# Row sums of two head pairs in one PSUM bank, with spreading products of 64 rows

## The chip, the cores and the metric

The kernel runs on one core of a Trainium2 chip. The core's engines work side by side, each through its own list of instructions in order, and wait for one another by semaphores: TensorE (PE in the profile; PEld is its weight load), VectorE (DVE), ScalarE (ACT), GpSimd (POOL) and SyncE (SP), which here issues nearly all transfers. The metric is the device time of one execution in microseconds (us). Three runs of the kernel before took 552.09, 552.25 and 552.89 us; the median is 552.25.

## The reference, cut to what matters

```
scores = scale * q @ k.T ; scores = cap * tanh(scores / cap)      # 2 batches x 12 heads, 448 x 64 each
attn   = exp(scores - max)
attn   = attn / (attn.sum(-1) + 1e-9)                             # the row sums of this case
x      = (attn @ v), heads joined to 768 columns
x      = moe(x)      # rms norm, silu(x @ w_gate) * (x @ w_val) @ w_out
out    = moe2(x)     # x @ w_in, leaky max with alpha, @ w_out
```

All is float32. The change touches only the attention and its passage into the first matrix products: how the exponentials of a row are summed, how 1/sum gets back to the partitions of the heads, and the order around these.

## The kernel before, in words

Two heads make a pair; there are 12 pairs, and pair i is prepared, scored and summed by the loop `for i in range(NPAIR)`, whose passes are called turns here. Turn i holds, on TensorE: the scores of pair i (`qk`, L207; four score groups, of which the narrow last one comes first, then three with two heads on 64 rows each), the row sums of pair i-1 (`sums`, L249) and its product with v (`pv`, L236). Values are split in a rounded high part and a rest (`hi`, `lo`), so that each score takes three products. ScalarE does tanh (L216) and exp (L221) of pair i into the tile `pt`.

The exponentials lie with the keys on the partitions, so a row sum is a product with ones. `sums` makes eight products of 32 columns per pair, in four column groups that run beside each other: two rounds. The result stands in a PSUM bank of its own (`under()`), and VectorE copies it out (`us`, L272, the *u-copy*). Two small transfers (`gt`, L275) bring the sums of a pair to 32 partitions. For each two pairs `recip` (L284 to L291, tiles gf, th, tl) adds the parts, takes the reciprocal and splits it, and two transfers (L295) put it into the tile r. `norm` (L322) then spreads it by a product with `sel_t` to 128 partitions, and VectorE multiplies it into the copied output of the pair (`ee`, L264, the *o-copy*; `xf`, L323).

Other work is strewn over the turns by a table of (turn, step): `a` puts a step behind the exp of its turn, `z` behind the output product. Such steps are `prep` (L190, L191: hi and lo of the next pair), and the conversion of the first weights: `w_load` (L102, 768 KB), `w_top` (L113), `w_bits` (L118, here *bits*, which frees the buffer of a load and so lets the next load go out), `w_hi` and `w_lo` (L133, L139; wh, wl), and sums of two weight tiles on GpSimd (L126). GpSimd also squares the outputs for the rms norm (L306, L310); in turn 9 TensorE adds the squares of the first batch over the partitions (`rms_sum`, L339). All orders are written out by hand: each engine does its steps in the order in which the code issues them.

PSUM banks set some of the waits: the spreads write into the banks `u` and `o`; `o` is also that of the output product, so a spread there needs the o-copy of pair i-2 to be done.

Of the kernel before, what the change touches and what calls it, by code (L numbers as in the profile page):

```python
# [34 lines left out]
RP = 16  # L35
Q = 32
K3 = KD // 2
# [20 lines left out]
def attn_moe_kernel(ctx: ExitStack, tc: tile.TileContext, units, qk_in, v, sel, w, gvec, alpha, out):  # L58
# [22 lines left out]
    half = aconst.tile([P, 2, D], F32, name="half")  # L81
    sel_t = aconst.tile([P, 2, P], F32R, name="sel_t")
# [158 lines left out]
    def tiles_of(i):  # L241
        return [pt[i][:, min(n, TILES - 1)] for n in range(TILES + 1)]
# [171 lines left out]
    with tc.manual_schedule():  # L414
# [7 lines left out]
        for h in range(2):  # L422
            nc.vector.memset(half[h * D:h * D + D, h], 1.0)
# [922 lines left out]
```

## Time and profile before

| | |
|---|---|
| median of 3 runs | 552.25 us |
| profiled execution | 552.85 us, span 551.1 us |
| TensorE, VectorE, ScalarE, GpSimd busy | 99%, 81%, 67%, 18% of the span |
| attention, from the first score to the last output product | 4.56 to 100.64 us |
| TensorE's granted clock | full in all slices |

The profile is of one execution; its times count from the start of the span. Busy shares are an average: in the attention part VectorE and ScalarE are busier than over the whole span. A row of the timeline gives start, duration, engine, line, operation, the tiles written and read, and in brackets how long the engine stood idle before and what ended that. Consecutive instructions of one form are merged (x2 and so on).

### The profile page before, as it was taken

What the parts mean: (1) busy time and instruction counts of PE and PEld (TensorE: products, weight loads), DVE (VectorE), ACT (ScalarE), POOL (GpSimd) and SP (SyncE); (2) the same over time, 40 slices, a digit from 0 to 9 for tenths busy, and PEclk for the clock granted to TensorE, in tenths of its full rate; (3) what the DMA queues carried; (4) which work ended last, traced back from release to release, by engine and by line L of the source; (5) the groups of instructions that cost most, each with busy time, mean ns of one, the idle gap of its engine ahead of it and who ended that gap; (6) DMA issues with size and microseconds to landing.
All of it is one profiled execution on the core that took longest, in us unless ns stands there. A gap on an engine that the chain in (4) does not pass through costs nothing.

```text
span 551.1 us, 7691 instructions
## 1 busy us (share of the span) xinstructions
PE 545.6 (99%) x3061; PEld 461.3 (84%) x3061; DVE 448.5 (81%) x511; ACT 370.6 (67%) x433; POOL 98.8 (18%) x54
## 2 busy tenths in 40 slices
PE   8999999999999999999999999999999999999997
PEld 5444544699999999999999999999999999999996
DVE  4698889898999967878889898979866899999242
ACT  7989999477766554576757554787967996467110
POOL 0034663300065231010000048101111000000000
PEclk9999999999999999999999999999999999999999
DMA  7756420400334534065510573005512267013022
GB/s 253 260 188 197 164 73 8 163 12 1 120 120 162 178 110 171 1 228 173 184 46 1 229 230 114 1 0 173 172 58 69 105 203 255 0 59 115 0 101 100
DMA packets 17316, 66.09 MB, mean 120 GB/s; under 512 B 3584, under 2 KB 5504, under 8 KB 17280
## 3 DMA queue, kind: packets, MB, share of 16 engines
q1 hardware_dynamic: 16746, 65.08, 34.9%
q8 instruction: 24, 0.39, 0.3%
q10 hardware_dynamic: 390, 0.39, 0.2%
q0 software_dynamic: 144, 0.13, 0.1%
q14 instruction: 12, 0.10, 0.1%
HBM read 62.66 MB, written 2.75 MB: 119 GB/s over the span
## 4 chain that ended last, share of the span: by engine, by line
PE 96%; DVE 1%; ACT 1%; DMA 1%; issue 0%; DVEq 0%
PE s L395 19%; PE x L395 13%; PE m L395 13%; PE s L775 9%; PE s L749 8%; PE x L775 7%; PE oo L236 6%; PE s L207 5%; PE x L749 4%; PE m L775 4%; PE rps L249 3%; PE m L749 2%; PE s L408 1%; PE m L408 1%; PE x L408 1%; ACT pt L221 1%
## 5 line engine op out<-in xcount | busy, mean ns | idle before, releaser
L133 ACT CAST wh<-wt 128x768 fp32r<-128x768 f32 x105 | 87.1, 832 | 66.4 <-PE s L775 24.9
L139 DVE TENSOR_TENSOR wl<-wt,wh 128x768 fp32r<-128x768 f32 x108 | 113.6, 1053 | 12.5 <-ACT wh L133 12.2
L126 POOL TENSOR_TENSOR wt<-wt 128x768 f32<-128x768 f32 x33 | 75.1, 2284 | 265.9 <-DVE wt L118 97.9
L113 ACT CAST top<-raw 128x768 f16<-128x768 bf16 x64 | 68.8, 1076 | 27.0 <-DMA raw<-w_in 11.7
L118 DVE SCALAR_TENSOR_TENSOR wt<-raw,top 128x768 uint32<-128x768 uint32 x68 | 69.8, 1028 | 1.5 <-ACT top L113 1.5
L395 PE MATMUL s<-xx,wh 128*128 128x448 f32 x264 | 63.5, 364 | 0.0
L395 PEld LDWEIGHTS s<-xx,wh 128*128 128x128 f32 x264 | 49.4, 187 | 4.6 <-issue 0.7
L395 PE MATMUL x<-xx,wh 128*128 128x448 f32 x204 | 49.9, 366 | 0.0
L395 PE MATMUL m<-xx,wh 128*128 128x448 f32 x204 | 49.5, 364 | 0.0
L619 DVE TENSOR_TENSOR xx<-b,xx 128x896 fp32r<-128x896 f32 (+1 forms) x40 | 48.8, 1228 | 0.6 <-ACT xx L632 0.6
L216 ACT ACTIVATE pt<-s,cinv 128x896 f32<-128x896 f32 (+1 forms) x48 | 41.1, 911 | 6.2 <-PE s L207 5.9
L395 PEld LDWEIGHTS x<-xx,wh 128*128 128x128 f32 x204 | 38.2, 188 | 3.5 <-issue 0.4
L395 PEld LDWEIGHTS m<-xx,wh 128*128 128x128 f32 x204 | 38.2, 187 | 3.0
L775 PE MATMUL s<-xx,wh 128*128 128x448 f32 x132 | 40.0, 362 | 0.0
L236 PE MATMUL oo<-pt,vt 128*32 128x448 f32 x384 | 38.5, 540 | 0.4 <-ACT pt L221 0.3
L221 ACT ACTIVATE pt<-pt,cap_t 128x3136 f32<-128x3136 f32 (+2 forms) x13 | 35.3, 2714 | 0.4
L395 PE MATMUL s<-xx,wl 128*128 128x448 f32 x132 | 33.8, 364 | 0.0
L236 PEld LDWEIGHTS oo<-pt,vt 128*32 128x32 f32 x384 | 12.2, 110 | 23.6 <-issue 21.4
L775 PE MATMUL x<-xx,wh 128*128 128x448 f32 x104 | 31.2, 362 | 0.0
L749 PE MATMUL s<-xx,wh 128*128 128x448 f32 x96 | 27.2, 364 | 0.0
L775 PEld LDWEIGHTS s<-xx,wh 128*128 128x128 f32 x132 | 24.7, 187 | 2.1
L775 PE MATMUL s<-xx,wl 128*128 128x448 f32 x72 | 26.5, 367 | 0.0
(223 smaller groups left out, 1119.0 us busy)
## 6 DMA issues: line engine op xcount, KB each, us to landing
raw<-w_in SPq DMA_DIRECT2D x68, 768.0 KB
rw<-qk_in SPq DMA_DIRECT2D x11, 480.0 KB
vt<-v_in SPq DMA_DIRECT2D x12, 256.0 KB
out<-b SPq DMA_DIRECT2D x2, 448.0 KB
out<-b SPq DMA_DIRECT2D x2, 224.0 KB
out<-e SPq DMA_DIRECT2D x1, 448.0 KB
out<-c SPq DMA_DIRECT2D x2, 224.0 KB
gt<-us SPq DMA_DIRECT2D x23, 3.5 KB
```

What stands on the lines that cost most here:

```text
L113: copy(top_of[u].bitcast(F16)[:, 1::2], raw_t[u].bitcast(BF16)[:, 4:4 * n + 4:4])
L118: nc.vector.scalar_tensor_tensor(out=f_t[u].bitcast(U32), in0=raw_t.pop(u).bitcast(U32)[:, 1:2 * n + 1:2], scalar=13, in1=top_of.pop(u), o ...
L126: add(out=t, in0=f_t[a], in1=f_t[b], op=op)
L133: copy(h_t[u], f_t[u].rearrange("p (k m) -> p k m", m=P))
L139: nc.vector.tensor_tensor(out=l_t[u], in0=f_t[u].rearrange("p (k m) -> p k m", m=P), in1=h_t[u], op=ALU.subtract)
L216: nc.scalar.activation(out=t[:, 2 * g:2 * g + w], in_=st.pop((i, g))[:, :w, :S], func=AF.Tanh, scale=cinv)
L221: nc.scalar.activation(out=t[:, done:to], in_=t[:, done:to], func=AF.Exp, scale=cap_t)
L236: nc.tensor.matmul(oo[i][q * Q:q * Q + Q, :S], vv[:, n, q % 2 * Q:q % 2 * Q + Q], t[:, min(n, TILES - 1), :], start=c == 0, stop=c == TG, ...
L395: nc.tensor.matmul(ps[:, r, c0:c1], lhs, rhs[:, c0:c1], start=first and n == 0, stop=n == len(mm) - 1, skip_group_check=True,)
L619: nc.vector.tensor_tensor(out=out, in0=a, in1=b, op=op)
L749: nc.tensor.matmul(dst[m], wt[:, kk * MB + m, :], x, start=first and u == 0 and kk == 0 and n == 0, stop=u == 1 and kk == 1 and n == 2, sk ...
L775: nc.tensor.matmul(dst[m], wt[:, kk * MB + m, :], x, start=start and ks + kk == 0 and i == 0, stop=fin and last and kk == 1 and i == 2, sk ...
```

## The change

- `sums` works for two pairs. All row sums of two pairs stand in one bank: each product has 32 columns of a strip that is zero but for eight of them, so the four rows of head sums of a column group don't touch. For the even pair VectorE first adds tiles 0, 1 to tiles 2, 3 (`add_halves`, tile tp, 128x896); the first half of that takes part in the even pair's four products, the second half is the first of the odd pair's eight: 12 products for 16.
- The bank is copied out once per two pairs, in the turns with even i, and one transfer of 16 rows in 8 pieces each brings it to 128 partitions. `recip` folds these to 64 and then 32 partitions: seven VectorE instructions for four.
- 1/sum goes to rows 0, 32, 64, 96 (and the rest to 1, 33, 65, 97) of r, and a spread is a product over 64 rows. In the loop the first spread of a turn follows the narrow score group, in the second bank of that group's tile, the second follows the first wide score group.
- Places: recip stands ahead of prep in all turns (before: behind it in turns 3, 5 and 7); wh and wl of the first two weights stand in turns 4 and 5 (before 3 and 4); the loads of the second and third weight are issued in turn 1; behind the loop the last spreads come three products later, and three products of the next block come ahead of the sum of squares.

```diff
-RP = 16
+RP = 8
 Q = 32
+UNIT = Q // 4
...
+    def add_halves(i):
+        t = half_sum[i] = sb.tile([P, 2, S], F32, tag="tp", name="tp", bufs=1)
+        nc.vector.tensor_tensor(out=t, in0=pt[i][:, 0:2], in1=pt[i][:, 2:4], op=ALU.add)
 
     def sums(i):
 
-        us[i] = ps_s.tile([P, 2, 512], F32, tag="s", name="us")[:, 0] if i == NPAIR - 1 else under()
-        for n, t in enumerate(tiles_of(i)):
-            q = n % 2 * D + n // 2 % 2 * Q
+        n, j = group[i]
+        t, at_ = pt[i], lambda h: (0, 3 * UNIT - (2 * j + h) * UNIT)
+        tail = (t[:, TILES - 1], (1, 3 * UNIT - 2 * j * UNIT))
+        whole = [(t[:, c], at_(c % 2)) for c in range(TILES - 1)]
+        if j == 0:
+            row_sum[n] = under()
+            x = half_sum[i]
+            half_sum[i] = [(x[:, h], at_(h)) for h in range(2)]
+            steps = [*whole[4:], tail, half_sum[i][0]]
+        else:
+            steps = [half_sum.pop(i - 1)[1], *whole, tail]
+        for q, (x, (k, c)) in enumerate(steps):
+            q0 = q % 4 * Q
             nc.tensor.matmul(
-                us[i][q:q + Q, :S], half[:, n % 2, :Q] if n > 5 else ones[:, :Q], t, start=n < 4, stop=n > 3,
+                row_sum[n][q0:q0 + Q, :S], strip[:, k, c:c + Q], x, start=j == 0, stop=j == 1 and q > 3,
                 skip_group_check=True,
             )
...
+    def evac_u(n, queue=nc.sync):
+
+        gt[n] = sb.tile([4 * Q, S // RP], F32, tag="gt", name="gt", bufs=1)
+        u = sb.tile([P, S], F32, tag="us", name="us", bufs=1)
+        nc.vector.tensor_copy(u, row_sum.pop(n)[:, :S])
+        queue.dma_start(out=gt[n], in_=u[0:P:UNIT].rearrange("r (p s) -> r p s", p=RP))
...
+        nc.vector.tensor_copy(f, t[2 * Q:])
+        nc.vector.tensor_tensor(out=f, in0=t[:2 * Q], in1=f, op=ALU.add)
+        nc.vector.tensor_copy(t[m], f[Q:])
         nc.vector.scalar_tensor_tensor(
-            out=f[m], in0=t[m, 0], scalar=eps_t[m], in1=t[m, 1], op0=ALU.add, op1=ALU.add
+            out=f[m], in0=f[m], scalar=eps_t[m], in1=t[m], op0=ALU.add, op1=ALU.add
         )
...
+    def spread(i, rps):
+        n, j = group[i]
+        rows = slice(j * D, j * D + D)
+        nc.tensor.matmul(rps[:, :S], sel_t[rows], r2[n % 2][rows], start=True, stop=True, skip_group_check=True)
+
+    def scaled(i, rps):
         b, p = divmod(i, NP)
-        nc.tensor.matmul(rps[:, :S], sel_t[:, j, :], r2[n % 2], start=True, stop=True)
         nc.vector.tensor_tensor(out=xf[b][:, p, :], in0=ee.pop(i), in1=rps[:, :S], op=ALU.mult)
...
+            if i % 2 == 0:
+                (a if i else z)(i and i + 1, add_halves, i)
...
             if i % 2 == 1 and i > 2:
-                steps.insert(i < 9, (recip, (i - 3) // 2))
+                steps.insert(0, (recip, (i - 3) // 2))
...
-        for n, j in ((3, 0), (4, 1), (9, 6)):
+        for n, j in ((4, 0), (5, 1), (9, 6)):
...
             if i:
-                evac_u(i - 1)
+                if i % 2 == 0:
+                    evac_u((i - 1) // 2)
```

How VectorE's list reads now in turn 7, from the o-copy (ee) on. Before:

```order
L264 COPY ee<-oo 128x448
L190 CAST hi<-rw 128x960
L191 TENSOR_TENSOR lo<-rw,hi 128x960
L284 SCALAR_TENSOR_TENSOR gf<-gt,eps_t 64x28
L287 RECIPROCAL gf<-gf 64x28
L290 CAST th<-gf 64x28
L291 TENSOR_TENSOR tl<-gf,th 64x28
L118 SCALAR_TENSOR_TENSOR wt<-raw,top_95 128x768
L272 COPY us<-rps 128x448
```

And of the change:

```order
L278 COPY ee<-oo 128x448
L246 TENSOR_TENSOR tp<-pt 128x896
L293 COPY gf<-gt 64x56
L294 TENSOR_TENSOR gf<-gt,gf 64x56
L295 COPY gt<-gf 32x56
L296 SCALAR_TENSOR_TENSOR gf<-gf,eps_t,gt 32x56
L299 RECIPROCAL gf<-gf 32x56
L300 CAST th<-gf 32x56
L301 TENSOR_TENSOR tl<-gf,th 32x56
L191 CAST hi<-rw 128x960
L192 TENSOR_TENSOR lo<-rw,hi 128x960
L119 SCALAR_TENSOR_TENSOR wt<-raw,top_95 128x768
```

The half-sum add and recip (gf to tl) now come ahead of prep (hi, lo) and bits (wt); the u-copy (us) is gone from this turn.

VectorE's list at the passage from turn 5 to turn 6, from bits to the products xf. Before:

```order
L118 SCALAR_TENSOR_TENSOR wt<-raw,top_95 128x768
L272 COPY us<-rps 128x448
L264 COPY ee<-oo 128x448
L323 TENSOR_TENSOR xf<-ee,rps 128x448 x2
L190 CAST hi<-rw 128x960
```

And of the change:

```order
L119 SCALAR_TENSOR_TENSOR wt<-raw,top_95 128x768
L134 CAST wh<-wt 128x768
L140 TENSOR_TENSOR wl<-wt,wh 128x768
L278 COPY ee<-oo 128x448
L335 TENSOR_TENSOR xf<-ee,s 128x448
L335 TENSOR_TENSOR xf<-ee,rps 128x448
```

wh and wl stand where the u-copy stood, ahead of the o-copy (ee) of turn 6.

TensorE's list at the beginning of turn 6, from the output product of turn 5. Before:

```order
L236 MATMUL oo<-pt,vt 32x448 x16
L322 MATMUL rps<-r_1_93,sel_t 128x448
L207 MATMUL s<-hi 128x448
L207 MATMUL s<-hi,lo 128x448
L207 MATMUL s<-lo,hi 128x448
L322 MATMUL rps<-r_1_93,sel_t 128x448
L207 MATMUL s<-hi 128x448 x2
L207 MATMUL s<-hi,lo 128x448 x2
L207 MATMUL s<-lo,hi 128x448 x2
L207 MATMUL s<-hi 128x448 x2
```

And of the change:

```order
L237 MATMUL oo<-pt,vt 32x448 x16
L208 MATMUL s<-hi 128x448
L208 MATMUL s<-hi,lo 128x448
L208 MATMUL s<-lo,hi 128x448
L331 MATMUL s<-r_1_93,sel_t 128x448
L208 MATMUL s<-hi 128x448 x2
L208 MATMUL s<-hi,lo 128x448 x2
L208 MATMUL s<-lo,hi 128x448 x2
L331 MATMUL rps<-r_1_93,sel_t 128x448
L208 MATMUL s<-hi 128x448 x2
```

The two spreads (from r by sel_t) each moved behind the next score group; the first writes into a tile of scores.

## Rows read from the trace of the kernel before

**Rows 1.** The page, part 4: the chain that ended last, by engine.

```profile
PE 96%; DVE 1%; ACT 1%; DMA 1%; issue 0%; DVEq 0%
```

**Rows 2.** Busy us of each engine (operations), clock, DMA share, GB/s, by stretch.

```profile
32.11:40.01 7.90, 7.90 (x76) 3.96 (x72) 7.83 (x10) 6.37 (x6) 4.18 (x3) 1.00 0.56 191
...
87.92:95.40 7.48, 7.48 (x74) 3.56 (x70) 6.67 (x13) 7.26 (x7) 0.15 (x1) 1.00 0.03 4
...
28.81:95.53 66.72, 66.50 (x599) 31.18 (x592) 58.23 (x79) 61.13 (x50) 32.96 (x21) 1.00 0.39 124
```

**Rows 3.** Timeline, TensorE, turns 3 and 6: start us, duration us, then the instruction.

```profile
27.46 1.32 PE L249 MATMUL rps<-pt,ones 128*32 128x448 f32 x10
...
28.99 3.19 PE L236 MATMUL oo<-pt,vt 128*32 128x448 f32 x32
...
48.40 0.37 PE L322 MATMUL rps<-r,sel_t 128*128 128x448 f32 x1
```

**Rows 4.** Timeline, VectorE, turns 4 to 6.

```profile
39.53 0.56 DVE L133 CAST wh<-wt 128x768 fp32r<-128x768 f32 x1
...
41.00 0.62 DVE L264 COPY ee<-oo 128x448 f32<-128x448 f32 x1
41.53 0.65 DVE L190 CAST hi<-rw 128x960 fp32r<-128x960 f32 x1
...
43.29 0.23 DVE L284 SCALAR_TENSOR_TENSOR gf<-gt,eps_t 64x28 f32<-64x28 f32 x1
43.56 0.32 DVE L287 RECIPROCAL gf<-gf 64x28 f32<-64x28 f32 x1
43.91 0.17 DVE L290 CAST th<-gf 64x28 fp32r<-64x28 f32 x1
...
44.23 0.94 DVE L118 SCALAR_TENSOR_TENSOR wt<-raw,top 128x768 uint32<-128x768 uint32 x1
...
47.62 0.62 DVE L264 COPY ee<-oo 128x448 f32<-128x448 f32 x1 [1.92 <-PE oo L236]
```

**Rows 5.** Timeline, SyncE (loads), VectorE and GpSimd, turns 4 to 8.

```profile
38.59 0.33 SPq L102 DMA_DIRECT2D raw<-w_in  x1
...
52.25 1.75 DVE L118 SCALAR_TENSOR_TENSOR wt<-raw,top 128x768 uint32<-128x768 uint32 x1
54.03 0.33 SPq L102 DMA_DIRECT2D raw<-w_in  x1
...
58.96 0.24 DVE L284 SCALAR_TENSOR_TENSOR gf<-gt,eps_t 64x28 f32<-64x28 f32 x1 [0.44 <-DMA gt<-us]
...
60.95 3.65 POOL L126 TENSOR_TENSOR wt<-wt 128x768 f32<-128x768 f32 x2 [4.13 <-DVE wt L118]
64.55 0.94 POOL L306 TENSOR_TENSOR sq<-xf 128x448 f32<-128x448 f32 x1
...
68.90 1.76 POOL L310 TENSOR_TENSOR s<-s,sq 128x448 f32<-128x448 f32 x1
```

**Rows 6.** Timeline, GpSimd, TensorE and VectorE, turns 9 and 10.

```profile
70.62 5.43 POOL L126 TENSOR_TENSOR wt<-wt 128x768 f32<-128x768 f32 x3
71.65 0.99 PE L339 MATMUL ms<-s,ones 128*128 128x448 f32 x2
...
73.22 1.07 DVE L284 SCALAR_TENSOR_TENSOR gf<-gt,eps_t 64x28 f32<-64x28 f32 x1
...
74.68 1.40 DVE L290 CAST th<-gf 64x28 fp32r<-64x28 f32 x1
...
80.02 0.36 PE L207 MATMUL s<-hi,lo 128*128 128x448 f32 x1
```

**Rows 7.** Groups by line and shape: busy us, mean ns of one, idle before.

```profile
L619 DVE TENSOR_TENSOR xx<-b,xx 128x896 fp32r<-128x896 f32 x34 | 36.5, 1085 | 0.0
...
L349 DVE RECIPROCAL spare<-spare 128x448 f32<-128x448 f32 x2 | 5.9, 2946 | 0.4 <-ACT spare L346 0.4
```

**Rows 8.** Timeline, ScalarE, turn 9.

```profile
73.50 2.80 ACT L216 ACTIVATE pt<-s,cinv 128x896 f32<-128x896 f32 x3 [1.20 <-PE s L207]
```

More of the change, by code (lines that the diff above doesn't have):

```diff
@@ L510, in attn_moe_kernel @@
                 evac_o(i - 2)
-            if pairs:
-                norm(i - 4, under())
             if i:
                 home = {1: (ps_r, "u"), 2: (ps_o, "o")}.get(i)
-                qk(i, TG, home[0].tile([P, 1, 512], F32, tag=home[1], name="s") if home else third())
-            if pairs:
-                norm(i - 3, upper("rps"))
+                t = home[0].tile([P, 1, 512], F32, tag=home[1], name="s") if home else third()
+                qk(i, TG, t)
+                if pairs:
+                    norms(i - 4, t[:, 1])
             if i == 9:
@@ L525, in attn_moe_kernel @@
                 qk(i, g, two())
+                if pairs and g == 0:
+                    norms(i - 3, upper("rps"))
                 if (i, g) == (1, 0):
@@ L551, in attn_moe_kernel @@
         evac_o(last - 1)
-        norm(last - 3, third()[:, 0])
-        norm(last - 2, under())
+        both = third()
+        norms(last - 3, both[:, 0], both[:, 1])
         sums(last)
@@ L556, in attn_moe_kernel @@
             square(j)
-        evac_u(last, (nc.sync, nc.scalar))
+        evac_u(len(members) - 1)
         pv(last)
@@ L580, in attn_moe_kernel @@
         w_hi(("g", 0, "S1"))
-        product(pb[1], ("g", 1, "A12"), "B21", True, rows=(0,), span=range(6))
-        norm(last - 1, under())
-        norm(last, third()[:, 0])
+        product(pb[1], ("g", 1, "A12"), "B21", True, rows=(0,))
+        norms(last - 1, under(), third()[:, 0])
         square(last - 1)
@@ L588, in attn_moe_kernel @@
         lows(late)
-        product(pb[1], ("g", 1, "A12"), "B21", True, rows=(0,), span=range(6, 3 * K3))
         sum4("g", 1)
         product(pb[1], ("g", 1, "A12"), "B21", True, rows=(1,))
+        pa[0] = chain_pair()
+        product(pa[0], ("g", 0, "A11"), "B11", True, rows=(0,), span=range(3))
         rms_sum(B - 1, upper("ms"))
@@ L668, in attn_moe_kernel @@
             keep_part(d11, g, pb, lambda: h_of(g)[:, 2:])
-            pa[g] = chain_pair()
-            product(pa[g], ("g", g, "A11"), "B11", True, cuts={} if g else {(0, 4): SHORT})
+            if g:
+                pa[1] = chain_pair()
+                product(pa[1], ("g", 1, "A11"), "B11", True)
+            else:
+                product(pa[0], ("g", 0, "A11"), "B11", True, rows=(0,), span=range(3, 3 * K3), cuts={(0, 4): SHORT})
+                product(pa[0], ("g", 0, "A11"), "B11", True, rows=(1,))
         w_hi(("g", 1, "S1"))
@@ L1290 @@
         va[:, :, h * TAIL:(h + 1) * TAIL, 6 + h] = vp[:, :, h, MAIN:]
-    se = np.zeros((P, 2, P), f32)
+    se = np.zeros((P, P), f32)
     for r in range(4):
-        for base in (0, 32):
-            se[base + r, r // 2, (r % 2) * D:(r % 2) * D + D] = 1.0
+        for x in range(2):
+            se[r * Q + x, (r % 2) * D:(r % 2) * D + D] = 1.0
     def tiles(a):
```

57 lines of the change are left out of this document (24 added, 33 removed).

## The prediction

> **What bounds the kernel now.** I read the page's engine shares and its chain first, then the attention part turn by turn, then each engine's timeline there. TensorE ends the program, 96% of the chain [rows 1]; its clock is granted in full in every stretch that I use [rows 2]. So every microsecond taken from TensorE is worth one, as long as nothing else becomes late. In the attention part the others have little to spare: from 28.81 to 95.53 us (66.72 us) VectorE is busy for 58.23, ScalarE for 61.13 [rows 2]. VectorE's largest idle stretch, 1.92 us at 47.62, ends when TensorE's output product is done [rows 4]: VectorE waits for TensorE, but only just.
>
> **TensorE's own sum.** The row sums of one pair are eight products in four column groups, two rounds: from 27.46 to the output products at 28.99, 1.53 us [rows 3], so 0.76 a round. Two pairs now take 12 products, three rounds for four: 6 x 0.76 = 4.6 us less. A turn with two spreads lasts 7.90 us, one without 7.48 [rows 2]: 0.21 a spread. If the two halves of 64 rows run beside other work, one of each two vanishes: 6 x 0.21 = 1.25 us (nothing if they don't). Together 5.8 us, were TensorE alone.
>
> **What VectorE pays.** Six half-sum adds of 128x896 are new, 1.09 us each by the adds of that shape [rows 7]. The u-copy falls away six times, 0.53 us each by the o-copy, which moves as much (41.00 to the next start at 41.53 [rows 4]). recip has seven instructions for four: the old four take 0.94 us, from 43.29 to 44.23 [rows 4]; the three new ones are near its small ones, 0.2 each; the reciprocal runs over 56 columns for 28, by 2946 ns for 448 against 0.32 us for 28 [rows 4, 7] 0.18 more, the others 0.03 each. Recip costs 1.8 us, 0.85 more (bounds: 0.3, if the small ones overlap, and 1.2). From turn 3 to turn 11 that is 5 x 1.09 + 5 x 0.85 - 5 x 0.53 = +7.0 us, where VectorE had 8.5 us idle (66.72 - 58.23), all of it waits for others. This sum alone forbids most of the 5.8 us: a gain of 1.5 us would need a VectorE that never waits.
>
> **Where it waits: turns 3 to 6.** Turn 3 gives up wh and wl (39.53 to 41.00 [rows 4], 1.47) and the u-copy, and takes the half-sum and the longer recip: 2.0 against 1.95, no change. Turn 4 has wh and wl of another weight, no change either. So VectorE comes to the o-copy of turn 5 at 41.0, as before [rows 4]; TensorE, faster, has waited for it. Turn 5's list is then: o-copy 0.53, half-sum 1.09, recip, prep 1.76 (41.53 to 43.29), bits 0.9, wh and wl 1.5 (moved here). Recip can't start before the transfer of the row sums has landed. That sits behind a weight load of 768 KB on SP's queue: the load of turn 6 was issued at 54.03, the transfer right behind it, and gf could start only at 58.96, having waited for it [rows 5]: 4.9 us after the load's issue. In turn 5 (load at 38.59) that allows 43.5, and the list is there at 42.6. So 43.5 + 1.8 + 1.76 + 0.9 + 1.5 = 49.4; I take 49.2, since in turn 5 of before gf started 4.7 after that load and did not wait [rows 4, 5]. The o-copy of turn 6 stood at 47.62 [rows 4]: +1.6. The second spread writes the bank that this copy empties; it moves from 48.40 [rows 3] to 50.0. The score group that used to follow it is done by then (-0.65): turn 7 starts at 55.38 + 1.6 - 0.65 = 56.3, 0.95 late. The transfer itself I price at the old one: one issue for two, 128 pieces for 64.
>
> **Turns 6 to 9.** After that o-copy VectorE's list is as before, so turn 6's bits end at 54.00 + 1.6 = 55.6, and the load goes out there. Recip of turn 7 now stands ahead of prep, and waits until 55.6 + 4.9 = 60.5, though VectorE is free at 58. Before, prep filled this time, and gf waited 0.44. Behind the waiting recip stand prep (hi and lo of pair 8, which TensorE needs at the start of turn 8) and bits, for which GpSimd waits. Recip ends at 62.3, prep at 64.05, bits at 64.95. TensorE wants lo at 56.3 + 6.72 + 0.3 = 63.3: 0.75 wait. Turn 9 then starts at 63.0 + 0.75 + 7.69 = 71.45 (before 70.74). GpSimd takes its two weight sums after these bits, then the squares of pairs 4 and 5: from 60.95 to 70.66, 9.7 us [rows 5], and TensorE's sum of squares in turn 9 needs the last of them. It came at 71.65, 1.0 after they were done [rows 6]. Now they end at 64.95 + 0.1 + 9.7 = 74.75, while TensorE is there at 72.35: 2.4 us wait (bounds: 0.1, if VectorE's prep and bits don't hold GpSimd up as they did before: its two sums take 3.65 and an undisturbed operation on squares 0.94 [rows 5], 3.65 + 4 x 0.94 = 7.4 for 9.7; 3.2, if the transfer of 128 pieces lands 0.8 later).
>
> **Turn 9 to the end.** In turn 9 VectorE copies the sum of squares and then has the half-sum and recip while GpSimd runs three weight sums (5.43 us). There gf took 1.07 us and th 1.40, against 0.23 and 0.17 undisturbed [rows 4, 6]: each waited until GpSimd's operation was over, 2.06 us in all. With GpSimd starting at 74.75, the half-sum goes at its first gap, 76.55 to 77.65; recip then takes 1.8 plus such waits. Two catches of a whole weight sum would be 3.6 us, none 0; I take the nearest row, 2.06. Prep ends at 77.65 + 1.8 + 2.06 + 1.76 = 83.3. TensorE's second score product of turn 10, at 80.02 before [rows 6], would come at 74.75 + 8.37 - 0.76 - 0.31 = 82.05: it waits to 83.3, +3.3 us.
>
> The Trainium skill ("SBUF — State Buffer", section "SBUF: two separate sides") says that VectorE and GpSimd share a port pair as an exclusive lock, taken also by a VectorE operation with two SBUF inputs, the loser blocking fully. The two rows of turn 9 agree (1.40 us against 0.17). By this rule the half-sum, which has two SBUF inputs, the first copy and the sum of recip would each lose to a weight sum, 3.6 us for my 2.06, and the time would be 1.5 us more than forecast; no row shows a copy of this size.
>
> From there: +0.6 (the second spread of turn 10 waits for an o-copy behind prep, bits 0.9 and wh 0.6), -0.2 (spreads), -0.76 (turn 11's sums), +0.5 of it back (ScalarE is busy 7.26 us in turn 11 [rows 2], and TensorE's turn would last 6.72), -0.2 and -0.2 for the last two pairs of spreads. 3.3 + 0.6 - 0.2 - 0.76 + 0.5 - 0.4 = +3.0. What follows keeps its places against TensorE; the three products put ahead of the last sum of squares fill what the later spread leaves, and I cost them at nothing (up to 0.6 if the last recip lands late). The profiled execution had 552.85 us (span 551.1), 0.6 above the median 552.25; its stretches are those of any run, so I add to the median: **555.3 us**.
>
> **Rivals.** *ScalarE is the only limit (chance 0.15).* If VectorE swallows its work, ScalarE's idle time bounds the gain: 66.72 - 61.13 = 5.6 us, of which 1.7 stays (1.20 in turn 9 behind the sum of squares [rows 8], and 0.5 of starts). 552.25 - 3.9 = 548.4. For it: TensorE's rounds go for certain. Against it: the 7.0 us of VectorE.
> *VectorE keeps pace, nothing gained (0.2).* The lag of turn 7 stands, but GpSimd's squares run unhindered in 7.4 us, and turn 9's wait goes, and some 0.4 of the catches with it: +3.0 - 2.4 - 0.4 = +0.2, 552.45 us. Against it: VectorE has the same hi, lo and bits to do among the squares.
> *The port decides (0.15).* Both small operations lose to a weight sum: +1.5, 556.8 us. It decides if recip of turn 9 starts before GpSimd's third sum does.
> *The change doesn't do what it says:* spreads of 64 rows do not overlap; then 1.25 us of TensorE's sum is missing, most of it hidden behind VectorE's waits, and 0.4 us is added. It is inside the range.
>
> **Numbers.** The forecast has 0.5. A measurement here can tell 0.2%, 1.1 us, from no change: faster is the first rival, 0.15; within is the second, 0.2; slower is the forecast and the third, 0.65. The range leaves out most of the first rival and a tail above the third: 551.0 to 557.6; the forecast's own is 553.6 to 556.4.
>
> **What would show it.** Right: recip's first copy in turn 7 waits 2 us or more on the transfer; TensorE waits on VectorE at the second spread of turn 6, on lo at turns 8 and 10, and on GpSimd at turn 9's sum of squares for over 1 us; rounds of row sums halve in odd turns. Wrong: recip finds its transfer landed; GpSimd's squares end ahead of turn 9; ScalarE without gaps through turns 5 to 11. Then the first rival holds.

## The result, and the profile after

The changed kernel takes 558.86 us (median of 4 runs, 558.30 to 559.01) against 552.17 before (4 runs, 552.02 to 552.89). By the medians it is 6.7 us slower, where 3.05 were forecast. The ratio on record is 1.0114, 95% interval 1.0101 to 1.0126, which is a loss of 5.6 to 7.0 us. Its profiled execution had 559.01 us and a span of 557.2; that of before 552.85 and 551.1. The spans differ by 6.1 us, and the account below explains these 6.1.

The page of the changed kernel: busy time, the clock in 40 slices, the chain [rows 1].

```profile
PE 545.3 (98%) x3013; PEld 460.0 (83%) x3013; DVE 458.6 (82%) x530; ACT 370.6 (67%) x433; POOL 99.6 (18%) x54
PEclk9999989999999999999999999999999999999999
PE 83%; DVE 8%; DMA 3%; ACT 2%; POOL 2%; issue 1%; DVEq 0%
```

TensorE held 96% of the chain, now 83%: VectorE, GpSimd and transfers have a share of it now. Up to turn 7 the steps came within 0.6 us of the forecast. Three rows of the timeline after (start, duration, instruction, idle before): the second spread of turn 6 waits for the o-copy (forecast start 50.0); ScalarE waits in that turn for the scaling, that is, for VectorE's product xf from the spread in the score tile, which was not in the forecast; and recip of turn 7 waits for its transfer (forecast 60.5).

```profile
49.46 0.46 PE L331 MATMUL rps<-r,sel_t 64*128 64x448 f32 x1 [1.19 <-DVE ee L278]
49.96 3.33 ACT L217 ACTIVATE pt<-s,cinv 128x448 f32<-128x448 f32 x4 [2.26 <-DVE xf L335]
60.14 0.19 DVE L293 COPY gf<-gt 64x56 f32<-64x56 f32 x1 [1.24 <-DMA gt<-us]
```

GpSimd's row of turns 8 and 9 answers to [rows 5, 6]: two weight sums, the squares (the last one is shown), three weight sums.

```profile
64.77 4.05 POOL L127 TENSOR_TENSOR wt<-wt 128x768 f32<-128x768 f32 x2 [6.83 <-DVE wt L119]
73.44 1.12 POOL L319 TENSOR_TENSOR s<-s,sq 128x448 f32<-128x448 f32 x1
74.53 6.23 POOL L127 TENSOR_TENSOR wt<-wt 128x768 f32<-128x768 f32 x3
```

The squares end at 74.56 (forecast 74.75, before 70.66), the weight sums at 80.76 (before 70.62 + 5.43 = 76.05 [rows 6]). VectorE in turn 9: the copy of the sum of squares, the half-sum, the first three of recip's seven steps, prep.

```profile
75.68 0.62 DVE L542 COPY spare<-ms 128x448 f32<-128x448 f32 x1 [2.98 <-PE ms L356]
76.22 1.08 DVE L246 TENSOR_TENSOR tp<-pt 128x896 f32<-128x896 f32 x1
77.33 1.70 DVE L293 COPY gf<-gt 64x56 f32<-64x56 f32 x1
79.07 1.77 DVE L294 TENSOR_TENSOR gf<-gt,gf 64x56 f32<-64x56 f32 x1
80.87 0.18 DVE L295 COPY gt<-gf 32x56 f32<-32x56 f32 x1
...
82.25 0.64 DVE L191 CAST hi<-rw 128x960 fp32r<-128x960 f32 x1
82.93 1.16 DVE L192 TENSOR_TENSOR lo<-rw,hi 128x960 fp32r<-128x960 f32 x1
```

The first two steps of recip take 1.70 and 1.77 us, though they take 0.19 and 0.21 in turn 7, where GpSimd rests; below, a step held like this is called *caught*. The third passes 0.1 us after GpSimd is done, and with it five steps (1.4 us) remain. In the kernel before, prep of pair 10 began here:

```profile
76.22 0.65 DVE L190 CAST hi<-rw 128x960 fp32r<-128x960 f32 x1
```

So prep is 6.03 us late. TensorE after: the sum of squares of turn 9, which waits for GpSimd's last square, the second score product of turn 10 (80.02 before [rows 6]), the first product behind the loop.

```profile
74.62 1.02 PE L356 MATMUL ms<-s,ones 128*128 128x448 f32 x2 [1.82 <-POOL s L319]
84.14 0.48 PE L208 MATMUL s<-hi,lo 128*128 128x448 f32 x1 [0.63 <-DVE lo L192]
106.09 1.04 PE L412 MATMUL s<-xx,wh 128*128 128x448 f32 x3
```

Before, that product started at 100.64: +5.45. Behind it to the end of the span there are 451.11 us, before 450.46: +0.65. Together 6.1, the difference of the spans. From prep to that product, busy us of the five engines, clock, DMA share, GB/s, after and then before:

```profile
82.25:106.09 23.84, 22.31 (x195) 8.79 (x187) 23.33 (x34) 20.20 (x19) 8.33 (x6) 1.00 0.06 16
```
```profile
76.22:100.64 24.42, 24.23 (x226) 9.88 (x219) 22.76 (x33) 21.50 (x19) 8.58 (x6) 1.00 0.07 14
```

Before, TensorE filled this stretch (24.23 of 24.42); after, VectorE does (23.33 of 23.84). The whole loss is thus 6.03 of late prep, less 0.58 in turns 10 and 11, plus 0.65 behind the loop. What made prep late took 18 more kernels to settle, because the first answers were wrong.

### The profile page after: what moved, and what is told of

Same layout as the page of the kernel before. It is cut to its first block, busy times and chain, and to the rows that moved or that the text cites. A ratio compares the mean times of both kernels' runs of the same rounds, so it can differ in the third digit from the quotient of the medians.

```text
span 557.2 us, 7578 instructions
## 1 busy us (share of the span) xinstructions
PE 545.3 (98%) x3013; PEld 460.0 (83%) x3013; DVE 458.6 (82%) x530; ACT 370.6 (67%) x433; POOL 99.6 (18%) x54
## 4 chain that ended last, share of the span: by engine, by line
PE 83%; DVE 8%; DMA 3%; ACT 2%; POOL 2%; issue 1%; DVEq 0%
PE s L412 18%; PE x L412 12%; PE m L412 12%; PE s L803 9%; PE s L777 8%; PE x L803 7%; PE x L777 4%; PE m L803 3%; PE m L777 2%; PE oo L237 1%; PE s L425 1%; ACT pt L217 1%; ACT pt L222 1%; DVE lo L192 1%; DVE hi L191 1%
## 5 line engine op out<-in xcount | busy, mean ns | idle before, releaser
L127 POOL TENSOR_TENSOR wt<-wt 128x768 f32<-128x768 f32 x33 | 76.3, 2321 | 268.5 <-DVE wt L119 100.6
L412 PEld LDWEIGHTS s<-xx,wh 128*128 128x128 f32 x264 | 49.3, 187 | 5.0 <-issue 0.9
L412 PE MATMUL s<-xx,wl 128*128 128x448 f32 x132 | 33.9, 365 | 0.0
L412 PE MATMUL x<-xx,wl 128*128 128x448 f32 (+1 forms) x104 | 26.6, 365 | 0.0
L412 PEld LDWEIGHTS s<-xx,wl 128*128 128x128 f32 x132 | 24.7, 188 | 2.2 <-DVE wl L140 0.3
```

What stands on the lines that cost most here:

```text
L127: add(out=t, in0=f_t[a], in1=f_t[b], op=op)
L412: nc.tensor.matmul(ps[:, r, c0:c1], lhs, rhs[:, c0:c1], start=first and n == 0, stop=n == len(mm) - 1, skip_group_check=True,)
```

## The experiments

Each kernel is the changed one with the edit shown. The table gives, from each run's trace, the end of GpSimd's weight sums of turns 8 and 9 (where they stand there), the start of prep of pair 10, the first product behind the loop, the span, and the median time with its ratio to before. The trace is of one execution, the time the median of 4 (11 in c6 and c7). Output products are named by their pair: that of pair n runs in turn n+1, and where an expectation says "the output product of turn 8", it is that of pair 8.

| run | sums end | prep | product | span | time, ratio |
|---|---|---|---|---|---|
| before | 76.05 | 76.22 | 100.64 | 551.1 | 552.2 |
| after | 80.76 | 82.25 | 106.09 | 557.2 | 558.86, 1.0114 |
| e1 | 79.96 | 81.46 | 105.26 | 556.4 | 558.36, 1.0114 |
| e2 | 80.65 | 82.14 | 106.06 | 557.1 | 558.79, 1.0115 |
| e3 | 79.24 | 80.73 | 104.57 | 555.7 | 557.12, 1.0086 |
| e4 | moved | 79.26 | 107.14 | 558.1 | 560.29, 1.0148 |
| e5 | 79.62 | 81.12 | 105.05 | 556.1 | 559.04, 1.0115 |
| e6 | 80.39 | 76.38 | 107.81 | 558.6 | 560.33, 1.0135 |
| e7 | 82.43 | 83.91 | 108.62 | 559.7 | 561.75, 1.0171 |
| e8 | 79.71 | 81.20 | 106.64 | 557.4 | 557.81, 1.0096 |
| e9 | 81.68 | 82.93 | 106.91 | 558.0 | 559.71, 1.0138 |
| e10 | 80.59 | 82.10 | 106.96 | 558.0 | 560.85, 1.0156 |
| c1 | 78.61 | 80.39 | 108.09 | 559.2 | 560.69, 1.0148 |
| c2 | 80.93 | 82.43 | 109.97 | 561.0 | 562.44, 1.0183 |
| e11 | moved | 79.28 | 104.78 | 559.7 | 560.73, 1.0141 |
| c3 | moved | 77.11 | 100.94 | 554.4 | 556.57, 1.0076 |
| c4 | 74.50 | 77.34 | 101.17 | 554.6 | 558.02, 1.0092 |
| c5 | 74.55 | 76.25 | 100.14 | 555.1 | 556.00, 1.0064 |
| c6 | 74.89 | 76.60 | 100.46 | 551.5 | 552.93, 1.0011 |
| c7 | 74.28 | 75.99 | 99.84 | 550.9 | 552.61, 1.0006 |

The first theory was: recip ahead of prep, the transfer behind the load, then TensorE's wait in turn 9 and the half clock that followed it. Theory 2, from e5 on, was: VectorE's own row of turn 9 ahead of prep sets the end, whatever is won before. The rivals are VectorE's added work as such (1) and ScalarE's waits for the scaling (2). Of the times that the theory under test led one to expect, only that of e3 came true; e5 and c6 missed theirs by 0.1 and 0.4 us, the others by more.

**e1.** Recip behind prep in turns 3 to 7.
```diff
-                steps.insert(0, (recip, (i - 3) // 2))
+                steps.insert(i < 9, (recip, (i - 3) // 2))
```


> Theory (the order around turns 7 to 9 costs most of it: the reciprocal chain ahead of prep waits 1.24 us for its transfer and itself takes about 2, so lo is written at 63.8, the weights' bits at 64.7, GpSimd's squares end at 74.6, TensorE waits 1.8 us in turn 9 and then runs at half clock for some 1.6 us): with the reciprocal chain behind prep in turns 3, 5 and 7, lo of turn 8 is there 2 to 3 us earlier, the wait of 1.8 us in turn 9 shrinks below 0.7, the granted clock stays at full, and the time falls by 2.5 to 4 us to about 555.5 us. Rival 1 (VectorE has 7 us more to do, wherever the chain stands): the wait moves to another place, 558 to 559.5 us. Rival 2 (ScalarE waits for the scaling of the first spread in turns 4, 6 and 8, since that spread lies in the score tile): no change, 558.9 us.


TensorE's wait in turn 9 fell from 1.82 to 0.41 us, as expected; the time did not follow (558.36).

**e2.** Eight products of ones in TensorE's wait.
```diff
-                rms_sum(0, upper("ms"))
+                ms = upper("ms")
+                for _ in range(8):
+                    nc.tensor.matmul(ms[:, :P], ones, ones, start=True, stop=True)
+                rms_sum(0, ms)
```


> Eight 128x128 products of ones are put ahead of turn 9's sum of squares, into its bank, where TensorE waits for GpSimd; nothing else is changed. Theory (of the 6.7 us, 1.6 are the half clock that follows this wait): the wait remains, but the granted clock stays near full from 74.6 to 79, the score products behind it run at 0.20 instead of 0.375 us, and the time falls by 1.2 to 1.8 us to about 557.3 us. Rival 1 and rival 2 (VectorE's work, ScalarE's waits): the work behind is due to other engines anyway, 558.6 to 559.2 us.


The clock stayed full in turn 9, and the half clock came in turn 10 instead, behind a wait of 1.52 us for hi (columns as above):
```profile
76.00:77.00 1.00, 1.00 (x14) 0.92 (x12) 1.00 (x2) 0.66 (x1) 1.00 (x2) 1.00 0.16 55
...
86.00:87.00 1.00, 1.00 (x9) 1.00 (x7) 0.69 (x2) 0.59 (x2) 0.54 (x1) 0.50 0.00 0
```
The output product of pair 8 came 1.7 us earlier, that of pair 9 0.9 later; the end did not move. So the half clock of turn 9 is not what makes prep late. That it costs nothing is not shown: of the changed kernel's four executions, the one whose mean granted clock was 1.000 took 558.30 us, the three below that 558.79 to 559.01; in e2 itself three at 1.000 took 558.37 to 559.02, the profiled one (0.996) 558.87.

**e3.** The weight load of even turns behind the row sums' transfer.
```diff
-                    a(i, w_next, conv[i - 2])
+                    (a if i % 2 else z)(i, w_next, conv[i - 2])
```


> In even turns the 768 KB weight load is issued behind the transfer of the row sums, instead of ahead of it. Theory: the reciprocal chains of turns 5 and 7 no longer wait 0.6 to 1.2 us for that transfer; in turn 7 the squares end some 1.2 us earlier, turn 9's wait falls from 1.8 to about 0.6 us and the clock may stay: 556 to 557.8 us. Rival 1 (VectorE's work as such): what the chain no longer waits it is late for otherwise, 558.5 to 559.2 us. Rival 2: 558.9 us.


1.5 to 1.7 us faster, the only early edit that paid. Recip of turn 9 was caught again, prep began at 80.73:
```profile
75.79 1.71 DVE L293 COPY gf<-gt 64x56 f32<-64x56 f32 x1
77.53 1.77 DVE L294 TENSOR_TENSOR gf<-gt,gf 64x56 f32<-64x56 f32 x1
...
80.73 0.64 DVE L191 CAST hi<-rw 128x960 fp32r<-128x960 f32 x1
```

**e4.** GpSimd's three weight sums of turn 8 in turn 10.
```diff
-        for put, n, fn, g in ((z, 6, sum1, 0), (z, 7, sum1, 1), (z, 7, sum2, 0), (a, 8, sum2, 1), (a, 8, sum3, 0),
-                              (z, 8, sum3, 1), (z, 10, sum4, 0)):
+        for put, n, fn, g in ((z, 6, sum1, 0), (z, 7, sum1, 1), (z, 7, sum2, 0), (z, 10, sum2, 1), (z, 10, sum3, 0),
+                              (z, 10, sum3, 1), (z, 10, sum4, 0)):
```


> GpSimd's three weight sums of turn 8 (6.2 us, 74.5 to 80.8) are put into turn 10, so that the reciprocal chain of turn 9 meets none of them. Theory (the two small operations that took 1.70 and 1.77 us in place of 0.19 and 0.21 were caught by these sums): they take 0.2 us each, the second score product of turn 10 starts 1 to 3 us earlier than 84.14, and the time falls by 0.6 to 2.5 us to about 557.5 us; if the sums in turn 10 catch other work there, half of it comes back. Rival 1 and rival 2: 558.7 to 559.2 us.


Recip of turn 9 was free (first row), the half-sum and recip of turn 11 were caught in its place, and TensorE waited for the rows they make:
```profile
77.41 0.19 DVE L293 COPY gf<-gt 64x56 f32<-64x56 f32 x1
...
93.48 2.44 DVE L246 TENSOR_TENSOR tp<-pt 128x896 f32<-128x896 f32 x1
95.95 1.72 DVE L293 COPY gf<-gt 64x56 f32<-64x56 f32 x1
```
```profile
102.09 0.47 PE L331 MATMUL s<-r,sel_t 64*128 64x448 f32 x2 [2.16 <-DMA r<-tl]
```

**e5.** wh and wl back in turns 3 and 4.
```diff
-        for n, j in ((4, 0), (5, 1), (9, 6)):
+        for n, j in ((3, 0), (4, 1), (9, 6)):
```


> wh and wl of the first two weight units are back where they were, in turns 3 and 4. Theory 2 (formed after the first four runs, in which turns 7 and 8 were won by up to 3 us and turn 9 gave nearly all of it back: VectorE's own row of turn 9, with the copy of the sum of squares, the half-sum add and the seven steps of the reciprocal chain ahead of prep, ends last and sets turn 10, whatever the turns ahead gain): the o-copy of turn 6 is 1.5 us earlier and ScalarE's wait of 2.26 us there goes, yet the end moves by 0 to 0.7 us only, 558.2 to 558.9 us. Rival 2 (ScalarE's waits): 1.5 to 2.3 us faster, 556.6 to 557.4 us.


Nothing in the median (559.04), though prep came 1.1 us earlier in the profiled execution. That one had 558.15 us at full clock; the other three (mean clock 0.996 to 0.997) had 558.85 to 559.46.

**e6.** Recip behind prep in every turn.
```diff
-                steps.insert(0, (recip, (i - 3) // 2))
+                steps.insert(1, (recip, (i - 3) // 2))
```


> The reciprocal chain stands behind prep in turns 5, 7, 9 and 11 alike (turn 9's stood ahead of it in both kernels). Theory 2: in turn 9 prep starts at about 76 instead of 80.8 to 82.3 us, TensorE no longer waits for lo in turn 10, the output product of turn 9 starts at 86.5 to 88 instead of 89.5 to 90 us, and the time falls by 2 to 3.5 us to about 556 us; should the spreads of turn 10 then wait for the two rows (they land some 2 us behind the chain's end), up to 1 us of it comes back. Theory 1 with rivals (VectorE's work as such, ScalarE's waits): as the run with the chain of turn 9 left ahead, 558.4 us.


Now prep was caught, and the first spread of turn 10 waited for the rows of recip:
```profile
76.38 2.30 DVE L191 CAST hi<-rw 128x960 fp32r<-128x960 f32 x1
78.71 2.69 DVE L192 TENSOR_TENSOR lo<-rw,hi 128x960 fp32r<-128x960 f32 x1
```
```profile
85.61 0.71 PE L331 MATMUL s<-r,sel_t 64*128 64x448 f32 x1 [3.47 <-DMA r<-tl]
```
Prep, caught in recip's place, ended 1.0 us behind GpSimd (81.40 against 80.39).

**e7.** No spread in the score tile.
```diff
-                    norms(i - 4, t[:, 1])
+                    pass
...
-                if pairs and g == 0:
-                    norms(i - 3, upper("rps"))
+                if pairs:
+                    norms(i - 4 + g, upper("rps"))
```


> Both spreads of an even turn go, one behind the first and one behind the second pair of score products, into the o bank; the score tile holds scores alone, so that its tanh waits for no scaling. Theory 2: ScalarE's waits of 1.48, 2.26 and 1.21 us in turns 4, 6 and 8 go, but turn 9 sets the end: 558 to 559.5 us. Rival 2 (these waits cost the time): 556 to 557 us. Against both, TensorE may wait at the second spread until the first is scaled, some 0.6 us in each of four turns: then 559 to 561 us.


ScalarE's waits for the scaling went, and the kernel was 2.9 us slower. By itself this does not refute rival 2, since the new place has a price of its own: TensorE waited 1.39 us at a spread of turn 6 for the o-copy, ScalarE 1.46 us for scores in that turn. What refutes it as the main cause is c6 below, where the waits for the scaling are still 2.47, 0.46 and 1.13 us in turns 4, 6 and 8 (changed kernel: 1.48, 2.26 and 1.21) and 5.9 us are back.

**e8.** The half-sum adds left out; TensorE's passes take a tile of ones.
```diff
-        t = half_sum[i] = sb.tile([P, 2, S], F32, tag="tp", name="tp", bufs=1)
-        nc.vector.tensor_tensor(out=t, in0=pt[i][:, 0:2], in1=pt[i][:, 2:4], op=ALU.add)
+        if i == 0:
+            half_sum["t"] = sb.tile([P, 2, S], F32, tag="tp", name="tp", bufs=1)
+            nc.vector.memset(half_sum["t"], 1.0)
+        half_sum[i] = half_sum["t"]
```


> The six half-sum adds (1.08 us each, more where GpSimd is busy) are left out: TensorE's passes take a tile of ones in place of the half sums, so that the row sums are other numbers; all else is the same. Theory 2 and rival 1 (VectorE's work): VectorE's row of turn 9 is 1.1 us shorter, that of the turns ahead too, and the time falls by 3 to 5.5 us to about 554.5 us. Rival 2 (ScalarE's waits): 0 to 1.5 us less. If the time falls below 552.4 us, the saved passes are worth what TensorE's rows say (5.8 us) and the adds alone turned the gain into a loss.


Six adds gone, 1.0 us faster in the median (557.81; the intervals of the two ratios overlap); prep again 1.49 us behind the sums. The work of the adds alone is not the loss. The profiled execution was the slowest of the four (559.18): TensorE ran at half clock from 85 to 91 us (one row; columns as in e2), and the product came 25.44 us behind prep in place of 23.84. The one at full clock took 556.69 us, 1.6 less than the changed kernel's at full clock (558.30).
```profile
86.00:87.00 1.00, 1.00 (x9) 0.39 (x9) 0.97 (x3) 1.00 (x3) 1.00 (x2) 0.50 0.00 0
```

**e9, e10.** In e9 the weight sums of turn 7 stand behind the squares; in e10 the copy of the sum of squares stands behind recip.
```diff
-        for put, n, fn, g in ((z, 6, sum1, 0), (z, 7, sum1, 1), (z, 7, sum2, 0), (a, 8, sum2, 1), (a, 8, sum3, 0),
+        for put, n, fn, g in ((z, 6, sum1, 0), (a, 8, sum1, 1), (a, 8, sum2, 0), (a, 8, sum2, 1), (a, 8, sum3, 0),
```
```diff
+        def keep_ms():
+            rms_keep(0)
+            nc.vector.tensor_copy(rstd[0], ms_of[0][:, :S])
+            ms_of[0] = rstd[0]
...
+            if i == 9:
+                steps.insert(1, (keep_ms,))
...
-                rms_keep(0)
-                nc.vector.tensor_copy(rstd[0], ms_of[0][:, :S])
-                ms_of[0] = rstd[0]
```


> GpSimd's two weight sums of turn 7 stand behind the squares of turn 8 instead of ahead of them; all else as in the changed kernel. Theory 2, now sharper: VectorE's copy of the sum of squares stands at turn 9's head and waits 3 us for GpSimd's squares; the half-sum add, the reciprocal chain and prep are queued behind it, so that lo of turn 10 is late by what the squares are late. Expected: the squares end near 71.5 instead of 74.6 us, neither TensorE (1.82 us) nor VectorE (2.98 us) waits for them, prep of turn 10 starts near 79.5 instead of 82.25 us, and the time falls by 2 to 3.5 us to about 556 us. Theory 1's first form (the clock and the wait of turn 9 are the cost): 1.8 to 3.4 us less as well, but with prep of turn 10 still past 81.5. Rivals 1 and 2: 558.3 to 559.3 us.

> VectorE's copy of the sum of squares stands behind the reciprocal chain of turn 9 and ahead of prep; GpSimd's order is as in the changed kernel, so that TensorE still waits 1.8 us for the squares. Theory 2: the half-sum add and the chain run in VectorE's idle 3 us (from 72.7 us), prep of turn 10 starts 2 to 3 us earlier, near 79.5 us, and the time falls by 1.5 to 3 us to about 556.5 us although TensorE's wait and the half clock behind it stay. Theory 1's first form: 558.3 to 559.3 us, since that wait is untouched.


Both slower. In e9 five weight sums ran on end, and three steps of recip were caught after the half-sum:
```profile
71.83 9.85 POOL L127 TENSOR_TENSOR wt<-wt 128x768 f32<-128x768 f32 x5
```
```profile
74.36 2.05 DVE L246 TENSOR_TENSOR tp<-pt 128x896 f32<-128x896 f32 x1
76.44 1.73 DVE L293 COPY gf<-gt 64x56 f32<-64x56 f32 x1
78.20 1.78 DVE L294 TENSOR_TENSOR gf<-gt,gf 64x56 f32<-64x56 f32 x1
80.02 1.71 DVE L295 COPY gt<-gf 32x56 f32<-32x56 f32 x1
```
In e10 recip began 3.0 us earlier (74.31), four steps were caught, and its last step came only 0.7 us earlier. Theory 2 falls: it is not recip's start that counts; GpSimd's last sum lets it end. The late copy brought a wait of its own, since the output products of pair 8 need that bank:
```profile
82.23 3.21 PE L237 MATMUL oo<-pt,vt 128*32 128x448 f32 x32 [1.41 <-DVE spare L487]
```

**c1, c2.** e3, e5 and e10 together; with e9 besides.


> Three edits at once: the row sums' transfer ahead of the weight load, wh and wl back in turns 3 and 4, the copy of the sum of squares behind the reciprocal chain. Theory 2: what the first two win ahead of turn 9 (1.5 and 1 to 1.5 us) is no longer eaten there: the output product of turn 8 starts near 76 us, that of turn 9 near 86, and the time is 552.5 to 555 us. If turn 9 is set by something that none of the three touches: above 556 us.

> The three edits of the run before and the squares ahead of the weight sums of turn 7. Theory 2: TensorE waits nowhere over 1 us in turns 8 to 10, its clock stays at full, the output product of turn 9 starts near 84.5 us, as in the kernel before, and the time is 550.5 to 553 us, level with the kernel before or a little faster. If VectorE's added 7 us of work are the limit by themselves (rival 1): 554 to 557 us.


Both slower. The wait of the output products of pair 8 for the late copy grew to 4.1 and 6.6 us. Read together, the table had by then the answer: prep started 1.25 to 1.51 us behind the end of the sums in ten of the eleven traces with the sums there and recip ahead of prep (c1, with its copy in between, 1.78). The first product behind the loop came 23.80 to 23.98 us behind prep in after, e1, e2, e3, e5 and e9, with 3 to 4 us at half clock in between (e1, e2, e3, e9) or none; it took longer in e7 (24.71), in e8 with its half clock (25.44), and in e10, c1 and c2 with the wait for the bank (24.86 to 27.70). Theory 3 is: each small step of recip passes only once per weight sum, so GpSimd's last sum sets recip's end, prep, and what follows.

**e11.** One of the three sums in turn 10, two behind the loop.
```diff
-        for put, n, fn, g in ((z, 6, sum1, 0), (z, 7, sum1, 1), (z, 7, sum2, 0), (a, 8, sum2, 1), (a, 8, sum3, 0),
-                              (z, 8, sum3, 1), (z, 10, sum4, 0)):
+        for put, n, fn, g in ((z, 6, sum1, 0), (z, 7, sum1, 1), (z, 7, sum2, 0),
+                              (z, 10, sum2, 1), (z, 10, sum4, 0)):
...
         sum4("g", 1)
+        sum3("g", 0)
+        sum3("g", 1)
```


> Of GpSimd's three weight sums of turn 8 one goes behind the squares of turn 10 and two behind the loop's end, past the last reciprocal chain; all else as in the changed kernel. Theory 3 (read from ten traces: prep of turn 10 starts 1.5 us behind the end of GpSimd's weight sums in all of them that have these sums there, whatever was done ahead, since each small step of the reciprocal chain passes only once per weight sum): the chain of turn 9 takes 1.9 instead of 4.9 us, prep starts near 79.3 instead of 82.25, the second score product of turn 10 near 80.6 instead of 84.14, turn 11's chain meets no sum either (in the run with all three in turn 10 it did), and the time falls by 2 to 3.5 us to about 556 us. Theory 2 (the copy of the sum of squares and the half-sum add ahead of it): 0 to 1 us less.


Prep at 79.28, as expected, but the product behind the loop only 1.3 us earlier, and 3.8 us were lost behind it; the time, about 556 expected, was 560.73.

**c3, c4, c5.** e3, e5 and e11 together (c3); the two sums of turn 7 behind the squares besides (c4); no half-sums for pairs 8 and 10 besides, 14 passes there (c5).


> That edit, the row sums' transfer ahead of the weight load, and wh and wl back in turns 3 and 4. Theory 3: with the chain of turn 9 free of GpSimd, what the other two win ahead of it (1.5 us and 1 us) stays: the output product of turn 9 starts near 85 us and the time is 552 to 554.5 us. Theory 2: 556 us or more.

> The three edits of the run before, and the two remaining weight sums of turn 7 behind the squares of turn 8. Theory 3: the squares no longer hold up TensorE at turn 9 (up to 1.8 us and the half clock behind it), but the two sums end near 75.5 us and catch the first steps of the chain; prep starts near 77 us at the earliest. Expected 551 to 553.5 us. Theory 2: as the run before, or 1 us less.

> The run before without the half sums of the last two groups (pairs 8 and 10): 14 passes there in place of 12, so TensorE has 0.76 us more in each of two turns and VectorE 1.08 us less. Theory 3 with VectorE as the limit of turns 9 to 11: up to 1 us faster than the run before. If TensorE is the limit there by then: up to 1.5 us slower.


The times missed the expectations: 556.57 in c3 (552 to 554.5 expected), 558.02 in c4, 556.00 in c5. In the loop theory 3 holds: the product came at 100.94, 101.17 and 100.14, against 106.09 and, before, 100.64. Of this start the parts had won 1.5 (e3), 1.0 (e5) and 1.3 us (e11) alone, and together 5.15 (c3; the traces of c3 and e5 have full clock throughout, the other two and the changed kernel's some 3 us at half): while GpSimd holds recip, earlier work wins little, and while GpSimd and TensorE are late, a free recip wins little. Behind the loop the moved sums did to the join of the squares what they had done in turn 9 to recip. In c5:
```profile
104.68 6.77 POOL L127 TENSOR_TENSOR wt<-wt 128x768 f32<-128x768 f32 x3 [4.41 <-DVE wl L140]
```
```profile
109.72 2.22 DVE L347 TENSOR_TENSOR sq<-sq 128x448 f32<-128x448 f32 x1
```
TensorE's second sum of squares waited for this join, in c3 and c5:
```profile
112.90 1.02 PE L356 MATMUL ms<-sq,ones 128*128 128x448 f32 x2 [2.06 <-DVE sq L345]
```
```profile
111.99 1.86 PE L358 MATMUL ms<-sq,ones 128*128 128x448 f32 x2 [2.08 <-DVE sq L347]
```
In c3 and c4 the clock stayed full behind this wait, and from the product to the end of the span it took 453.46 and 453.43 us; in e11 and c5 it fell to 0.50 for some 3 us, and it took 454.92 and 454.96. Here the half clock cost 1.5 us.

**c6, c7.** c5 with the two sums from behind the loop under VectorE's long reciprocal (c6, the edit against c5); wh and wl at the ends of turns 4 and 6 besides (c7).
```diff
-        sum3("g", 0)
-        sum3("g", 1)
...
         w_lo(("g", 0, "S1"))
+        w_sum(("g", 0, "S3"), ("g", 0, "A22"), ("g", 0, "S2"), ALU.subtract, home=("g", 0, "S1"))
+        sum3("g", 1)
         rms_tail(B - 1)
```


> As the run with four half sums, but the two weight sums that stood behind the loop's end (and there held up VectorE's join of the squares, for which TensorE waited 2.1 us) wait until wl of the first S1 unit is written, and so run under VectorE's reciprocal of the second sum of squares (2.95 us). Theory 3: the loop ends as in that run (the output product of turn 11 starts near 96.4 us, 1.1 us ahead of the kernel before), behind the loop the time is again the changed kernel's (some 0.6 us more than before), so 551 to 552.5 us: level with the kernel before or just ahead of it, and 6.4 to 7.9 us faster than the changed kernel. If the 5 us lost in turns 7 to 11 came from elsewhere and only moved behind the loop: above 554 us.

> The same with wh and wl of the first two units at the ends of turns 4 and 6 instead of 3 and 4, where they no longer stand ahead of the o-copy of an even turn (ScalarE's wait of 2.5 us in turn 4 goes). Expected: turn 4 is 1.1 us shorter; if prep of turn 8 (1.5 us later) still has its slack, the time is 0.5 to 1.1 us below the run before, 550.3 to 551.8 us; if lo of turn 8 is then late, no gain or up to 1 us slower.


```profile
108.76 0.63 DVE L347 TENSOR_TENSOR sq<-sq 128x448 f32<-128x448 f32 x1 [0.17 <-ACT sq L319]
...
111.70 2.95 DVE L368 RECIPROCAL spare<-spare 128x448 f32<-128x448 f32 x1 [0.38 <-ACT spare L365]
```
```profile
111.47 3.66 POOL L127 TENSOR_TENSOR wt<-wt 128x768 f32<-128x768 f32 x2 [3.63 <-DVE wl L140]
```
The join takes 0.63 us again, and the reciprocal loses nothing beside two sums (2.95 us; 2946 ns in the kernel before [rows 7]). 552.93 (interval of the ratio 1.0002 to 1.0020) and 552.61 (0.9997 to 1.0015): 5.9 and 6.3 us of the 6.7 are back, and neither beats the kernel before. These 5.9 us are not GpSimd's alone: e3, e5 and, for the last two groups, the loss of the half-sums are in them. In c7 the output product of pair 3 starts 1.5 us earlier than in c6 (turn 4 is 1.2 us shorter, 1.1 expected of the place of wh and wl); 0.3 us of it is left in the time. In c6's stretch from prep to the product TensorE is the limit again:
```profile
76.60:100.46 23.86, 23.86 (x218) 10.08 (x212) 22.65 (x33) 22.11 (x20) 10.90 (x7) 1.00 0.06 16
```

## Why the forecast was wrong

The direction and the mechanism up to turn 9 were right: VectorE's o-copy of turn 6 (48.78, forecast 49.2), the wait of recip for its transfer, bits late, GpSimd's squares to within 0.2 us, TensorE's wait in turn 9 (2.4 forecast, 1.82). Of the signs one was smaller than named: recip of turn 7 waited 1.24 us, not 2 or more, because the half-sum ahead of it took 2.09 us for 1.09. The size was off in three terms, set against the 6.1 us by which the spans differ.

- **Recip's waits in turn 9: "I take the nearest row, 2.06".** They cost 1.70 + 1.77 in place of 0.19 + 0.21, 3.1 us, so 1.0 more than the term; recip started 0.3 us earlier than forecast, and its other steps and prep were 0.1 us longer. Lo of pair 10 was there at 84.09 (forecast 83.3), and the second score product came 4.1 us late in place of 3.3: +0.8. The step behind the term was wrong in kind: I priced each catch as an event of its own. e9 and c2 show that each small step passes once per weight sum, so that recip's end is tied to the end of GpSimd's row. That row gives the 6.03 us by which prep is late: the sums end 4.71 us later than before (3.82 of it the late bits of turn 7, 0.80 slower sums, 0.09 the squares), and the steps left behind them take 1.3 us more. The third rival had both catches and its 556.8 us, nearer but 2.1 us short of the median; it too counted catches and did not tie recip's end to GpSimd's.
- **Turns 10 and 11: +0.6 at the second spread, then -0.2, -0.76, +0.5, -0.2 and -0.2, in all -0.3.** From the second score product of turn 10 to the first product behind the loop it took 21.95 us (106.09 - 84.14), before 20.62: +1.33. I counted there what TensorE saves, while VectorE, with half-sum, longer recip and the rest, was busy for all but 0.5 of the 23.84 us from prep to that product. The sum of VectorE's work (+7.0 us), worked out ahead, belonged into this term.
- **"What follows keeps its places":** +0.65 for 0.

3.3 + 0.8 = 4.1, and 4.1 + 1.33 + 0.65 = 6.1. (The forecast's own +3.0 was 3.3 - 0.3; the measured +1.33 stands in the place of the -0.3.)

The Trainium skill ("SBUF — State Buffer", section "SBUF: two separate sides") calls the port pair of VectorE and GpSimd an exclusive lock, whose loser blocks fully. The copy of 1.70 and the add of 1.77 us agree, and by that rule the forecast would have been nearer (556.8). My choice of the middle row against it was the mistake.

The rival with ScalarE as the only limit and the one in which VectorE keeps pace are refuted by 1.0101 as the interval's lower end. The change does on TensorE what it says. The four products of the even pair's sums took 0.78 us in turn 5 (42.09 to 42.87), where a pair's eight took 1.53; and the spreads of 64 rows run beside other products: in turn 4 they started at 31.98 and 32.71 and the score groups behind them 0.01 and 0.15 us later, before 0.31 and 0.30.

That these savings come to nothing even in c6 and c7 is only partly explained. 0.6 us lies behind the loop. The rest is lost by turn 9, since the output product of pair 8 starts at 75.98 in c6 (all but its first part at 76.38), hardly ahead of 76.13 before. From one output product to the next, turns 5 and 7 are 0.73 us shorter in c6 than before, which is the round that the sums save there, but turns 4, 6 and 8, those with the spreads, are 1.47, 0.42 and 1.08 us longer. In these ScalarE waits for the scaling (2.47, 0.46 and 1.13 us, a term that the forecast does not have), and TensorE waits 0.81 us for the o-copy in turn 4 and 0.80 us for the rows of r in turn 8. Which of these waits costs the time was not tried on c6 or c7, and no run took VectorE's longer recip away; this stays open.

## What to carry to other kernels

Before an operation is split into several small ones on VectorE, look what GpSimd runs at that time: where the small ones are held as here, their number counts, not their size, and the last of them ends behind GpSimd's last operation. Where several engines are near their limit, an undo of one part shows little, because the next limit stands right behind; follow one late event (here the start of prep of pair 10) through all traces instead of the total. A long operation that the two engines do side by side without loss, as the reciprocal here, is the place to put GpSimd's sums.

## What the runs showed of the hardware

Beside GpSimd's weight sums, operations of very different size on VectorE took nearly the same time. In c2 four steps of recip on end took 1.73, 1.76, 1.71 and 1.75 us, alone 0.19, 0.21, 0.18 and 0.27; the half-sum of 128x896 took 2.05 us in e9, alone 1.08. The last two steps in c2:
```profile
77.49 1.71 DVE L295 COPY gt<-gf 32x56 f32<-32x56 f32 x1
79.24 1.75 DVE L296 SCALAR_TENSOR_TENSOR gf<-gf,eps_t,gt 32x56 f32<-32x56 f32 x1
```
GpSimd's three sums took longer too: 6.23 us in the changed kernel, 5.43 before [rows 6]. And TensorE's clock: behind the wait of 1.82 us in turn 9 the changed kernel ran at 0.50 (1.2 of 2.4 GHz) from 76 to 79 us. In e5 a wait of nearly the same length (1.78 us) at the same place was followed by full clock:
```profile
77.00:78.00 1.00, 1.00 (x10) 0.88 (x8) 0.97 (x2) 0.89 (x1) 1.00 (x1) 0.50 0.00 0
```
```profile
73.44 1.02 PE L356 MATMUL ms<-s,ones 128*128 128x448 f32 x2 [1.78 <-POOL s L319]
```
```profile
76.00:77.00 1.00, 1.00 (x14) 0.40 (x14) 0.97 (x2) 1.00 (x2) 1.00 (x1) 1.00 0.00 0
```
The first row is of the changed kernel, the other two of e5. What tells the two cases apart was not tried; behind the loop the same difference cost 1.5 us (c3 and c4 against e11 and c5).
